# Idle products from a program constant, and three tile shapes changed, in a fused sketch-attention and ELU feed-forward kernel

## The chip, the cores and the metric

The kernel runs on one core of a Trainium2 chip. The metric is device time in microseconds of a whole execution. The kernel before took 266.83 us, the median of three runs (266.22 to 266.89).

A core has five engines that run their own instruction lists: TensorE (matrix products; PE in the profile, and PEld for its loads of the stationary operand), VectorE (DVE), ScalarE (ACT), GpSimd (POOL) and SyncE (SP), which here only issues DMAs. Semaphores order them.

## The reference

Polynomial sketch attention over 4 batches, 4 heads, 1088 positions and head size 32, then a feed-forward block of width 2048 with ELU:

```python
def phi(x):
    a = np.einsum('rd,bhsd->bhsr', S1, x)
    b = np.einsum('rd,bhsd->bhsr', S2, x)
    return np.einsum('bhsi,bhsj->bhsij', a, b).reshape(*x.shape[:-1], r * r)   # r = 8
q_p, k_p = (phi(q), phi(k))
kv = np.einsum('bhsf,bhsd->bhfd', k_p, v)
z = np.sum(k_p, axis=2)
num = np.einsum('bhsf,bhfd->bhsd', q_p, kv)
den = np.einsum('bhsf,bhf->bhs', q_p, z)[..., None] + 1e-06
attn = num / den
# x = attn with heads side by side: 4352 x 128
h = x @ w_in                                   # 4352 x 2048
g = np.where(h > 0.0, h, np.exp(np.minimum(h, 0.0)) - 1.0)
out = g @ w_out                                # 4352 x 128
```

All of it is float32 at the chip; S1, S2 and the two weight matrices arrive as 64-bit floats and are rounded to 32 bits on the chip by integer operations.

## The kernel before

**The whole.** The 4352 rows are cut into nine groups `g` of 512 rows (the last one has 256), and the hidden width into 8 pairs `cp` of 128 columns. A step `(g, cp)` computes h for one group and one pair on TensorE (`mm1`, L841), ELU on ScalarE and VectorE (`elu`), and, two steps later, the product with w_out (`mm2`, `mm2_blocks`, or `mm2_seven`, which forms a block product from seven smaller ones whose sums GpSimd makes). `steps` lists 64 such steps; the last, smaller group has a loop of its own at the end. Attention work for later groups is put between them by tables: `at(n, ...)` right behind step n's `mm1`, `mid` and `late` further behind. The order is the program's own: each engine runs its list as written, since the schedule is manual.

**Tile shapes.** TensorE's array can be used whole (128 columns of the stationary operand) or as narrower column tiles, and also cut by rows. In the profile `128*32` means 128 rows and 32 columns of the stationary operand. A float32 product appears as two matrix instructions and two loads. `quarters` (L256) issues one product as column tiles of width `width[0]`, which is 32 up to step 30 and 64 from there on; `mm2_seven` (L767) and `mm2_blocks` use the same width.

**Start.** Behind the program's opening barrier VectorE fills a tile `some` with 1.0 (L88, L89). TensorE multiplies `some` with itself into the bank `idle` in `keep_warm` (L261, L263): nothing reads the results. Three such products of 256 columns and one of 128 (L296, L297) come first. Then TensorE makes `sps` and `SXps` from the sketches Sx (L299, L285), the features of the first batch's keys `abp` (`KF`, L338), their sums `zps` (`z_tile`, L416), and the features of the first queries `abqp` (`q1_first`, L513).

**z of the first batch.** ScalarE copies the sums to `zl`. `Z` (L441) multiplies them with SXh by `quarters`, in four 32-wide tiles; VectorE masks the result into `SW` (L447). An idle product of 96 columns follows (L959), and then `zqp` (`q1z_first`, L525), which reads `SW`. From `zqp` VectorE makes the denominators and the query features (`pw`, `den`, `an`, `qp`), and goes on with rounding the first weights (`RC_2`, L193: L118, L122, L130, L138). Later batches call `Z` through `turn` (L1038).

**First feed-forward product.** TensorE transposes the query features (`qtp`), multiplies them with kv (`xps`), makes the features of the second group (`abwp`, L534), and runs an idle product of 192 columns (L974). Then `mm1_first` (L848) begins the feed-forward work with 32-wide tiles.

**Step 30.** The loop over the steps sets `width[0] = 64` ahead of step 30's `mm1` (L1103 to L1105). Behind that `mm1`, `queries(4, 6, 31)` (L699) runs products in 32*32 tiles that don't use `quarters`, and then comes `mm2_seven` of step 28.

Of the kernel before, what the change touches and what calls it, by code (L numbers as in the profile page):

```python
# [12 lines left out]
F32 = mybir.dt.float32  # L13
# [14 lines left out]
def kernel(  # L28
# [21 lines left out]
    nc = tc.nc  # L50
    B, H, S, D = q.shape
    R = S1.shape[0]
    P = 128
# [10 lines left out]
    const = ctx.enter_context(tc.tile_pool(name="const", bufs=1))  # L64
# [20 lines left out]
            src = v[b].rearrange("h (y t) d -> y h t d", t=NT)[:, :, t0:t1, :]  # L85
            eng.dma_start(vt[b][r, :VN].rearrange("p (h t d) -> p h t d", h=H, t=KT)[:, :, :t1 - t0, :], src)

    some = const.tile([P, 256], F32, name="some")  # L88
    nc.vector.memset(some[:], 1.0)  # L89
    idr = const.tile([P, 2 * R, R], F32, name="idr")  # L90
    nc.vector.memset(idr[:], 0.0)
    Sx = const.tile([P, H, D], F32, name="Sx")
# [157 lines left out]
    idle = psum.tile([P, 512], F32, name="idle", tag="o0", bufs=1)  # L250
# [2 lines left out]

    width = [32]

    def quarters(dst, lhs, rhs, **kw):  # L256
        for c in range(0, P, width[0]):
            nc.tensor.matmul(dst[c:c + width[0]], lhs[:, c:c + width[0]], rhs, skip_group_check=True,  # L258
                             tile_position=(0, c), **kw)

    def keep_warm(n, cols=256):  # L261
        for i in range(n):
            nc.tensor.matmul(idle[:, :cols], some[:, :P], some[:, :cols], skip_group_check=True)  # L263


    nc.gpsimd.tensor_copy(idr[:R], _ap(ident[:R, :R], [[0, 2 * R], [1, R]]))
# [14 lines left out]
    SXh = const.tile([P, FD], F32, name="SXh")  # L281
# [12 lines left out]
    SWq = const.tile([FD, B, 2, 4, R], F32, name="SWq")  # L294
    SWs = const.tile([FD, B - 1, 4, R], F32, name="SWs")
    keep_warm(3)  # L296
    keep_warm(1, 128)  # L297
    sps = psum.tile([P, 512], F32, name="sps", tag="aux")
    nc.tensor.matmul(sps[:, :2 * R], Sx[:].rearrange("p h d -> p (h d)"), ident[:, :2 * R])  # L299
    make_SXh()  # L300
# [102 lines left out]
    def KO_first(t0, t1):  # L403
        half, o = divmod(t0, 5)
        n = t1 - t0
        a_ = kf_ps[half][:, 64 * o:64 * (o + n)].rearrange("p (m x r) -> p m x r", x=2, r=R)[:, :, 1, :]
        b_ = feats[0][:, 0, t0:t1].rearrange("p t h r -> p (t h) r")
        nc.vector.tensor_mul(feats[0, half][:, o:o + n].rearrange("p t h i j -> p (t h) i j"),
                             _ap(a_, list(a_.ap[1:]) + [[0, R]]), _ap(b_, [[R, n * H], [0, R], [1, R]]))
# [30 lines left out]

    def Z(b, ps, zl):  # L441

        quarters(ps[:, 96:128], SXh[:], zl[:])

    def Z_out(b, ps):
        z = wzs[b] = SW[:, :, 2, :] if b == 0 else work.tile([FD, H, R], F32, name="wz", tag="wz")[:]
# [8 lines left out]
    def KV(b, ps):  # L455
        for f in range(2):
            quarters(ps[:, 128 + P * f:128 + P * f + P], kvz[b][:, f].rearrange("p c s -> p (c s)"), ident[:])
# [11 lines left out]
    def Z_first():  # L469
        ps = psum.tile([P, 512], F32, name="zps", tag="h", bufs=4)  # L470
        for i in range(KT):
            z_tile(0, ps, i)
        return ps, ZC(0, ps)
# [46 lines left out]
    def q1z_first():  # L520
        p = psum.tile([P, 512], F32, name="zqp", tag="h", bufs=4)
        for i in range(4):
            for u in range(2):
                b, t = half_tile(0, 2 * i + u)
                nc.tensor.matmul(p[64 * u:64 * u + 64, i * 32:i * 32 + 32].rearrange("p (h r) -> p h r", h=H),  # L525
                                 qT[b][:, t, :], SW[:, :, 2, :], skip_group_check=True, tile_position=(0, 64 * u))
        return p[:, :128].rearrange("p (t h r) -> p h t r", t=4, h=H)

    def q1_second():
        p = psum.tile([P, 512], F32, name="abwp", tag="h", bufs=4)  # L530
        for i in range(4):
            for u in range(2):
                b, t = half_tile(1, 2 * i + u)
                nc.tensor.matmul(p[64 * u:64 * u + 64, i * 96:i * 96 + 96], qT[b][:, t, :],  # L534
                                 SW[:].rearrange("p h x r -> p (h x r)"), skip_group_check=True,
                                 tile_position=(0, 64 * u))
        abw[1] = work.tile([P, H * 4, 3 * R], F32, name="abw1", tag="abq1", bufs=1)
        nc.scalar.copy(abw[1][:].rearrange("p (h t) y -> p h t y", h=H),
                       p[:, :384].rearrange("p (t h y) -> p h t y", t=4, h=H))
# [185 lines left out]
    def seven(g, cp):  # L725
        return 2 <= g < NQ - 1 or g == 1 and cp >= NP - 2
# [13 lines left out]
    def sums7(g, cp, c):  # L740
        if c == 0:
            ts[g, cp] = work.tile([P, 4, 2, P], F32, name="tt", tag="raw", bufs=5)
        t = ts[g, cp]
        b11, b12 = (quarter(g, cp, 0, y) for y in range(2))
        if c == 0:
            nc.gpsimd.tensor_tensor(t[:, 0], b12, b11, op=SUB)  # L746
            return
        b21, b22 = (quarter(g, cp, 1, y) for y in range(2))
        nc.gpsimd.tensor_tensor(t[:, 2], b22, b12, op=SUB)  # L749
        nc.gpsimd.tensor_tensor(t[:, 1], t[:, 2], b11, op=ADD)  # L750
        nc.gpsimd.tensor_tensor(t[:, 3], b21, t[:, 1], op=SUB)  # L751
# [40 lines left out]
    def fin_seven_copy(g):  # L792
        a = acc[g][0]
        sa = sas[g] = work.tile([P, 2, P], F32, name="sa", tag="sa", bufs=1)
        if g == 1:
            nc.scalar.copy(sa[:, 0], acc[g][1][:, :P])
            return
        nc.scalar.copy(sa[:].rearrange("p k s -> p (k s)"), a[:, P:3 * P])
# [42 lines left out]
    def mm1(g, cp, cs=(0, 1)):  # L841
        n = qn[g] * P
        if 0 in cs and (g, cp) not in hs:
            hs[g, cp] = [psum.tile([P, 512], F32, name="h", tag="h", bufs=4) for c in range(2)]
        for c in cs:
            quarters(hs[g, cp][c][:, :n], W[:, cp, c * P:c * P + P], xg[g][:, :n])

    def mm1_first():  # L848
        hs[0, 0] = [psum.tile([P, 512], F32, name="h", tag="h", bufs=4) for c in range(2)]
        for w in range(2):  # L850
            for c in range(2):
                cols = [x[:].rearrange("p (m w s) -> p w m s", w=2, s=P)[:, w] for x in (hs[0, 0][c], xg[0])]
                quarters(cols[0], W[:, 0, c * P:c * P + P], cols[1])

    def elu_a(g, cp, c, parts=(0, 1)):

        n = qn[g] * P
        if c == 0 and 0 in parts:
            es[g, cp] = work.tile([P, 2, 512], F32, name="e", tag="e", bufs=2)
        e = es[g, cp][:, c, :n]  # L860
        if 0 in parts:
            nc.scalar.activation(e, hs[g, cp][c][:, :n], RELU, scale=-1.0)  # L862
        if 1 in parts:
            nc.scalar.activation(e, e, EXP, scale=-1.0)  # L864

    def elu_d(g, cp, c):
        n = qn[g] * P
        if c == 0:
            gs[g, cp] = work.tile([P, 2, 512], F32, name="gg", tag="gg", bufs=3)
        nc.vector.scalar_tensor_tensor(gs[g, cp][:, c, :n], es[g, cp][:, c, :n], -1.0, hs[g, cp][c][:, :n],  # L870
                                       op0=ADD, op1=MAX)

    def elu(g, cp, c):
        elu_a(g, cp, c)
        elu_d(g, cp, c)

    def mm2(g, cp, first, last):
        n = qn[g] * P
        if first:
            ops[g] = psum.tile([P, 512], F32, name="o", tag=f"o{g % 2}", bufs=1)  # L880
        gg = gs.pop((g, cp))
        for c in range(2):
            quarters(ops[g][:, :n], W[:, cp, (2 + c) * P:(3 + c) * P], gg[:, c, :n],
                   start=(first and c == 0), stop=(last and c == 1))
# [66 lines left out]
    zps, zl = Z_first()  # L951
# [4 lines left out]
    Z(0, zps, zl)  # L956
    Z_out(0, zps)
    KO_first(7, KT)
    keep_warm(1, 96)  # L959
    zq = q1z_first()  # L960
    q2_den(0, zq)
    RA(0)
# [8 lines left out]
    RC_2()  # L971
    q5_early(0)
    q1_second()
    keep_warm(1, 192)  # L974
    mm1_first()
    RA(2)
    RB(2)
# [122 lines left out]
    N = len(steps)  # L1100
    for n in range(2, N):
        g, cp = steps[n]
        if n == 30:  # L1103
            width[0] = 64
        mm1(g, cp)  # L1105
        for f, *a in extra.get(n, ()):
            f(*a)
        elu(g, cp, 0)
        if seven(g, cp):
            sums7(g, cp, 0)  # L1110
        for f, *a in extra.get((n, 0), ()):
            f(*a)
        before = steps[n - 2]
        ends = n > 3 and seven(*before) and before[1] == NP - 1
        if ends:
            elu_a(g, cp, 1, (0,))
            mm2_seven(*before, False, True)
            fin_seven_copy(before[0])
            elu_a(g, cp, 1, (1,))
            fin_seven_a(before[0])  # L1120
            if before[0] == 1:
                fin_seven_b(1)
            elu_d(g, cp, 1)
        else:
            elu(g, cp, 1)
        if seven(g, cp):
            sums7(g, cp, 1)
        if ends and before[0] > 1:
            fin_seven_b(before[0])
        for f, *a in extra.get((n, 1), ()):  # L1130
            f(*a)
        g, cp = before
        if seven(g, cp):
            if cp < NP - 1:
                mm2_seven(g, cp, cp == (NP - 2 if g == 1 else 0), False)
        elif g == 1:
            mm2_blocks(cp)
        elif n > 2:
            mm2(g, cp, cp == 0, cp == NP - 1)
            if cp == NP - 1:  # L1140
                fin1(g)
# [55 lines left out]
```

## Time and profile before

| | us |
|---|---|
| median of three runs | 266.83 |
| the runs | 266.22 to 266.89 |
| profiled execution | 266.17 |
| its span, first to last instruction | 264.4 |
| TensorE busy | 258.8 (98%) |
| VectorE busy | 188.5 (71%) |
| ScalarE busy | 184.5 (70%) |
| GpSimd busy | 167.3 (63%) |
| idle products on TensorE (14 instructions) | 1.19 to about 16.3, of the span's first 16.3 |

Times in the profile count from the span's start. A line of the timeline gives start, length, engine, line of the kernel, operation, what it writes and reads, shape and count; brackets at its end tell how long the engine was idle before it and what released it. Matrix products are pipelined and their ends are modelled, so the distance between starts says more than a length. "Idle products" in this text are the ones of `keep_warm`; "idle time" is time in which an engine does nothing.

### The profile page before, as it was taken

Reading aid. Unit: us, or ns where it says so; the run is one execution under the profiler, and the core shown is the slowest. Engines: PE = TensorE matmul, PEld = TensorE weight load, DVE = VectorE, ACT = ScalarE, POOL = GpSimd, SP = SyncE. Lnnn points to the kernel's source line nnn. Section 1 sums busy time; section 2 is a strip of 40 time slices with the busy share of each in tenths; the row PEclk is TensorE's granted clock in tenths of the full one; section 3 lists DMA queues with packets and bytes.
Section 4 is the critical chain, followed back from the end, with each engine's and each line's share of the span. In section 5 each row is a group of like instructions: output and inputs, shape, how many; then the busy total and the mean of one; then the engine's idle time right before and its main releaser. Section 6 shows DMA issues by size and latency. Waiting matters only on the chain.

```text
span 264.4 us, 9711 instructions
## 1 busy us (share of the span) xinstructions
PE 258.8 (98%) x4115; PEld 160.6 (61%) x4115; DVE 188.5 (71%) x349; ACT 184.5 (70%) x356; POOL 167.3 (63%) x247
## 2 busy tenths in 40 slices
PE   8899999999999999999999999999999999999994
PEld 7652334354346666667666666665766666667994
DVE  6899999997969997996567675644446445673651
ACT  2469978677567556785587777776777777777792
POOL 4400008203279996798858799898688888998310
PEclk9999999999999999999999999999999999999999
DMA  6997089011011110001100110011001100110021
GB/s 176 333 347 212 2 252 249 6 40 49 2 22 22 29 22 2 2 4 22 26 2 0 24 22 0 2 15 29 3 2 20 24 1 2 18 17 10 2 34 28
DMA packets 26442, 13.73 MB, mean 52 GB/s; under 512 B 19328, under 2 KB 24576, under 8 KB 26400
## 3 DMA queue, kind: packets, MB, share of 16 engines
q1 hardware_dynamic: 25968, 12.76, 18.9%
q8 instruction: 32, 0.52, 0.8%
q10 hardware_dynamic: 368, 0.30, 0.3%
q14 instruction: 10, 0.08, 0.1%
q0 software_dynamic: 64, 0.07, 0.1%
HBM read 10.88 MB, written 2.23 MB: 50 GB/s over the span
## 4 chain that ended last, share of the span: by engine, by line
PE 97%; DVE 1%; ACT 0%; issue 0%; DVEq 0%
PE h L258 44%; PE pb L787 16%; PE pa L787 13%; PE o L258 5%; PE pb L763 4%; PE ol L258 3%; PE idle L263 2%; PE kv L425 1%; PE h L681 1%; PE qps L681 1%; PE kfps L357 1%; PE abp L338 1%; PE qps L573 1%; PE qtp L631 1%; PE kv L258 1%; PE xps L638 0%
## 5 line engine op out<-in xcount | busy, mean ns | idle before, releaser
L258 PE MATMUL h<-xg,W 128*32 128x512 f32 (+3 forms) x896 | 130.7, 539 | 0.0
L870 DVE SCALAR_TENSOR_TENSOR gg<-e,h 128x512 f32<-128x512 f32 x128 | 85.5, 680 | 54.3 <-ACT e L864 50.8
L862 ACT ACTIVATE e<-h 128x512 f32<-128x512 f32 x128 | 75.5, 590 | 46.4 <-PE h L258 42.7
L864 ACT ACTIVATE e<-e 128x512 f32<-128x512 f32 x128 | 80.9, 632 | 3.8
L258 PEld LDWEIGHTS h<-xg,W 128*32 128x32 f32 (+1 forms) x896 | 42.2, 122 | 43.2 <-issue 35.8
L749 POOL TENSOR_TENSOR tt<-gg 128x256 f32<-128x256 f32 x50 | 37.0, 740 | 15.4 <-DVE gg L870 15.1
L746 POOL TENSOR_TENSOR tt<-gg 128x256 f32<-128x256 f32 x50 | 36.7, 734 | 7.8 <-DVE gg L870 7.3
L750 POOL TENSOR_TENSOR tt<-tt,gg 128x256 f32<-128x256 f32 x50 | 37.5, 750 | 3.9
L751 POOL TENSOR_TENSOR tt<-gg,tt 128x256 f32<-128x256 f32 x50 | 37.1, 743 | 3.9
L787 PEld LDWEIGHTS pa<-gg,W 128*64 128x64 f32 (+1 forms) x496 | 23.8, 125 | 23.5 <-issue 22.9
L787 PE MATMUL pa<-gg,W 128*64 128x128 f32 (+1 forms) x496 | 30.5, 274 | 0.0
L787 PE MATMUL pb<-tt,SS 128*64 128x128 f32 (+1 forms) x480 | 29.5, 273 | 0.0
L787 PEld LDWEIGHTS pb<-tt,SS 128*64 128x64 f32 (+1 forms) x480 | 22.6, 126 | 0.0
L787 PE MATMUL pa<-tt,SS 128*32 128x128 f32 (+1 forms) x288 | 21.1, 273 | 0.0
L135 POOL TENSOR_TENSOR raw<-raw,tiny 128x512 f32<-128x512 f32 x1 | 1.0, 1041 | 29.9 <-DVE raw L130 29.9
L787 PE MATMUL pb<-gg,SS 128*64 128x128 f32 (+1 forms) x256 | 19.8, 273 | 0.0
L787 PE MATMUL pb<-tt,W 128*64 128x128 f32 (+1 forms) x256 | 19.8, 273 | 0.0
L258 PE MATMUL o<-gg,W 128*32 128x512 f32 x128 | 15.3, 594 | 0.0
L787 PEld LDWEIGHTS pa<-tt,SS 128*32 128x32 f32 (+1 forms) x288 | 13.5, 123 | 0.3 <-POOL tt L750 0.3
L787 PEld LDWEIGHTS pb<-gg,SS 128*64 128x64 f32 (+1 forms) x256 | 12.6, 125 | 0.0
L787 PEld LDWEIGHTS pb<-tt,W 128*64 128x64 f32 (+1 forms) x256 | 12.6, 125 | 0.0
L763 PE MATMUL pb<-gg,W 128*32 128x256 f32 x192 | 11.5, 380 | 0.0
(164 smaller groups left out, 279.6 us busy)
## 6 DMA issues: line engine op xcount, KB each, us to landing
raw<-in_moe_w_in_dram SPq DMA_DIRECT2D x8, 256.0 KB, 6.8
raw<-in_moe_w_out_dram SPq DMA_DIRECT2D x8, 256.0 KB, 6.8
hd_k<-in_k_dram SPq DMA_DIRECT2D x3, 544.0 KB, 6.8
hd_q<-in_q_dram SPq DMA_DIRECT2D x3, 544.0 KB, 8.0
out_dram<-ob SPq DMA_DIRECT2D x88, 16.0 KB, 1.5
v<-in_v_dram SPq DMA_DIRECT2D x4, 288.0 KB, 6.3
v<-in_v_dram SPq DMA_DIRECT2D x4, 256.0 KB, 8.1
hd_k<-in_k_dram SPq DMA_DIRECT2D x1, 288.0 KB, 3.4
```

What stands on the lines that cost most here:

```text
L258: nc.tensor.matmul(dst[c:c + width[0]], lhs[:, c:c + width[0]], rhs, skip_group_check=True, tile_position=(0, c), **kw)
L263: nc.tensor.matmul(idle[:, :cols], some[:, :P], some[:, :cols], skip_group_check=True)
L681: nc.tensor.matmul(ps[w][s * r:s * r + s, 64 * k:64 * (k + m)], lhs, qpT[g, i][rows, o + 2 * k:o + 2 * (k + m), f, :], start=(f == 0 and j ...
L746: nc.gpsimd.tensor_tensor(t[:, 0], b12, b11, op=SUB)
L749: nc.gpsimd.tensor_tensor(t[:, 2], b22, b12, op=SUB)
L750: nc.gpsimd.tensor_tensor(t[:, 1], t[:, 2], b11, op=ADD)
L751: nc.gpsimd.tensor_tensor(t[:, 3], b21, t[:, 1], op=SUB)
L763: nc.tensor.matmul(acc[1][0][r:r + width[0], 256 * hi:256 * hi + 256], lhs[:, w:w + width[0]], gg[:, c, 256 * u:256 * u + 256], start=(cp ...
L787: nc.tensor.matmul(bank[r:r + width[0], P * col:P * col + P], lhs[:, w:w + width[0]], rhs[:, u], start=(first and i in ((0,) if g == 1 els ...
L862: nc.scalar.activation(e, hs[g, cp][c][:, :n], RELU, scale=-1.0)
L864: nc.scalar.activation(e, e, EXP, scale=-1.0)
L870: nc.vector.scalar_tensor_tensor(gs[g, cp][:, c, :n], es[g, cp][:, c, :n], -1.0, hs[g, cp][c][:, :n], op0=ADD, op1=MAX)
```

## The change

Four edits. `some` and its memset go, and `keep_warm` reads a constant 1.0 that the program writes ahead of its opening barrier, repeated over 128 partitions and 256 columns by its access pattern. `keep_warm` gets a tile width: the 96-column product is issued in two 64-wide tiles, the 192-column product in 32-wide ones, the others as before; the last of the first four has 224 columns instead of 128. `quarters` can be given a width, and `Z` gives it 64 for the first batch. The step to `width[0] = 64` stands behind step 30's `mm1` and `queries` instead of ahead of them.

```diff
-    some = const.tile([P, 256], F32, name="some")
-    nc.vector.memset(some[:], 1.0)
...
-    def quarters(dst, lhs, rhs, **kw):
-        for c in range(0, P, width[0]):
-            nc.tensor.matmul(dst[c:c + width[0]], lhs[:, c:c + width[0]], rhs, skip_group_check=True,
+    def quarters(dst, lhs, rhs, tile=None, **kw):
+        tile = tile or width[0]
+        for c in range(0, P, tile):
+            nc.tensor.matmul(dst[c:c + tile], lhs[:, c:c + tile], rhs, skip_group_check=True,
                              tile_position=(0, c), **kw)
-    def keep_warm(n, cols=256):
+    def keep_warm(n, cols=256, tile=P):
+        ones = nc.const_aps.tensor(1.0, [P, 256], F32)
         for i in range(n):
-            nc.tensor.matmul(idle[:, :cols], some[:, :P], some[:, :cols], skip_group_check=True)
+            for c in range(0, P, tile):
+                nc.tensor.matmul(idle[c:c + tile, :cols], ones[:, :tile], ones[:, :cols], skip_group_check=True,
+                                 tile_position=(0, c))
...
     keep_warm(3)
-    keep_warm(1, 128)
+    keep_warm(1, 224)
...
-        quarters(ps[:, 96:128], SXh[:], zl[:])
+        quarters(ps[:, 96:128], SXh[:], zl[:], None if b else 64)
...
-    keep_warm(1, 96)
+    keep_warm(1, 96, 64)
...
-    keep_warm(1, 192)
+    keep_warm(1, 192, width[0])
...
-        if n == 30:
-            width[0] = 64
         mm1(g, cp)
         for f, *a in extra.get(n, ()):
             f(*a)
+        if n == 30:
+            width[0] = 64
         elu(g, cp, 0)
```

## The prediction

> **What bounds the kernel now.** I read the page's chain of waits first. By engine it is "PE 97%; DVE 1%", so TensorE sets the end. Page part 1:
>
> ```profile
> PE 258.8 (98%) x4115; PEld 160.6 (61%) x4115; DVE 188.5 (71%) x349; ACT 184.5 (70%) x356; POOL 167.3 (63%) x247
> ```
>
> Then busy time by stretches. TensorE is busy 111.59 of the 111.60 us from 16.30 to 127.90, and 4.30 of 4.30 in the next 4.30. So what arrives early at 16.3 stays early, and time taken out of TensorE's list after that is taken from the end. Before 16.3 short pieces hand over between engines, and each must be asked what released it. From the timeline of all engines, two places ahead of 16.3:
>
> ```profile
> 0.87 0.27 DVE L89 MEMSET some<- 128x256 f32 x1 [0.87 <-PEq L1182]
> 1.19 3.36 PE L263 MATMUL idle<-some 128*128 128x256 f32 x8 [1.19 <-DVE some L89]
> ...
> 4.34 0.45 PE L299 MATMUL sps<-ident,Sx 128*128 128x16 f32 x2
> ...
> 7.95 0.69 PE L513 MATMUL abqp<-Sab,qT 128*64 128x64 f32 x16
> ...
> 8.56 0.27 PE L258 MATMUL zps<-zl,SXh 128*32 128x32 f32 x8
> 8.76 0.46 PE L263 MATMUL idle<-some 128*128 128x96 f32 x2
> 8.97 0.19 DVE L447 TENSOR_TENSOR SW<-zps,bmask 128x32 f32<-128x32 f32 x1 [0.55 <-PE zps L258]
> 9.21 0.66 PE L525 MATMUL zqp<-SW,qT 128*64 128x32 f32 x16
> ```
>
> Columns: start, length, engine. Idle products wait for the memset of `some`. `sps` follows them, although its input Sx is ready at 3.71 + 0.28 = 3.99. VectorE waits 0.55 us for z, and zqp follows SW.
>
> ```profile
> 14.94 0.88 PE L534 MATMUL abwp<-SW,qT 128*64 128x96 f32 x16
> ...
> 15.39 0.69 DVE L138 SCALAR_TENSOR_TENSOR W<-raw,W 128x512 f32<-128x512 f32 x1
> ...
> 15.75 0.59 PE L263 MATMUL idle<-some 128*128 128x192 f32 x2
> ...
> 16.27 1.93 PE L258 MATMUL h<-xg,W 128*32 128x256 f32 x32
> ```
>
> The first feed-forward product (16.27) follows the idle one; its weights are rounded by 16.08. The third place is step 30, with two rows from an earlier stretch for comparison (TensorE alone):
>
> ```profile
> 35.50 1.90 PE L258 MATMUL h<-xg,W 128*32 128x512 f32 x16
> 37.33 0.71 PE L357 MATMUL kfps<-kT,Sxp 64*32 64x288 f32 x16
> ```
>
> ```profile
> 127.32 0.44 PE L787 MATMUL pa<-tt,SS 128*32 128x128 f32 x8
> 127.53 0.44 PE L787 MATMUL pb<-tt,W 128*32 128x128 f32 x8
> 127.91 1.94 PE L258 MATMUL h<-xg,W 128*64 128x512 f32 x8
> 129.77 0.41 PE L681 MATMUL h<-qpT,kvs 32*32 32x128 f32 x2
> ```
>
> Read starts, not lengths: ends overlap. Eight 128x128 products in one tile shape are 0.21 to 0.22 us start to start; the last eight before 127.91 take 0.38.
>
> **What the Trainium skill says.** "TensorEngine Tiling (Array Packing)", Key Properties: "Changing tiling mode (not just tile) drains the TensorE". It gives no price. The trace agrees and prices it: h to pb in one shape is 39.72 to 41.43 = 1.71 us, h to kfps in another shape 1.83, so 0.12. I use 0.10 where the group ahead is short, since the tiles of an h group start spread over about 0.02. "TensorE: Matmul & The Clock Gate", section What's actually happening: the clock rises after a busy window of about 3.4 us that runs free of the program. The page's clock row shows full speed from the start, so it doesn't show the rise. Durations do: loads of abp average 213 ns in 5.2 to 6.0 us and 141 ns after, and 256-column idle products last 634 ns (median, first group) against 380 at 11.6. I find no page on an operand that repeats one element.
>
> **The change part by part.**
>
> *First products.* The constant 1.0 is written at 0.28 to 0.38, before the opening barrier; other engines' first work after it starts at 0.74 to 0.87. Taking 0.78 for TensorE, the start comes 0.41 earlier. The group grows by 96 columns in each of two passes. Cold, 128 columns cost 634 - 421 = 213 ns, or 1.66 ns each; 192 cost 0.32. So `sps` moves from 4.34 to 0.78 + 3.15 + 0.32 = 4.25, by 0.09. Sab waits behind a kT transpose that starts at 4.58 on landed data, and is little earlier than 4.83, but abp (5.33) starts in the drain behind SXps and can use most of the 0.09. While the clock is still low, half of that is lost if the rise (about 6.0) stays put: 0.05. Bounds: 0 where kT's transposes (to 6.36) pace abp, 0.5 where the rise comes a window sooner. The memset off VectorE is worth nothing: the queue waits for `ident` and then for S at 2.31. If the rise came late instead, abp's pace (213 against 141 ns) would cost up to 0.9.
>
> *z in 64-wide tiles.* Neighbours abqp and zqp are 64 wide. Four shape changes (abqp, z, idle, zqp) go. The one ahead of z is on the path: 0.10. z also has four products instead of eight: about 0.02. The idle pair keeps its columns (two tiles, two passes of 96, about 0.08 each by abwp's pace of 0.81 us for eight such pairs less the drain); it would end near 8.7 and is hidden by the wait for SW, with 0.3 to spare. So SW, zqp, pw: 0.11 earlier (0.08 to 0.2). VectorE then runs unbroken from pw at 9.99 to W at 16.08, with no row released by a DMA, and carries the 0.11.
>
> *Idle 192 in 32-wide tiles.* Eight products instead of two, same columns: at h's pace (1.71 us for four rounds of 512) two rounds of 192 are 0.32, and 0.03 for the first loads. The change ahead of it remains, the one behind goes: TensorE is free at 15.75 + 0.35 = 16.10 instead of 16.27. But W ends at 16.08, and TensorE took 0.12 from VectorE's end (qp, 12.90) to its loads (13.02) at a like wait, so 16.20. Gain 0.07 (0 to 0.17) on top of the 0.11. What is late next is VectorE's rounding.
>
> *Step 30.* mm1 stays 32 wide behind 32-wide products; queries are 32*32 either way and seven-product blocks 64 wide behind them either way. Before: 127.53 to 129.77 = 2.24. After: 0.22 for the last eight, 1.83 for h with its change: 2.05. Gain 0.19 (0.09 if only one drain counts). Issue is dearer, 16 products for 8, but 1.71 to 1.72 us in both widths when no change intervenes (133.75 to 135.47 is 64 wide). The queries' data are ready: qpT at 127.15, SWs at 127.98.
>
> No part adds a wait or a DMA or passes SP's queue; one wait goes, at TensorE's first load.
>
> Sum: 0.05 + 0.11 + 0.07 + 0.19 = 0.42. The profiled execution took 266.17 (span 264.4, 1.8 around it), so 265.75 for it. It stands at the low edge of the runs, 266.22 to 266.89, which may be the clock's window falling differently. Against the median the sum gives 266.41. I take 266.25, between the two: a start 0.41 earlier also moves the whole spread of clock rises.
>
> **The rivals.**
>
> *The clock rises a window sooner (about 266.0 or less).* Speaking for it: 0.41 is 12% of a 3.4 us window, and the longer fill leaves less gap. Against: the present rise already comes 4.8 us after the start. Worth 0.4 to 0.5 more, bounded by kT's transposes: 0.9 in all, 265.3 to 266.0.
>
> *The gains don't reach the end (266.7).* W gates 16.2, ScalarE is back to back from about 20 to 30, and pb waits for its copy at 30.3. For it: that wait. Against: ScalarE's row starts behind qtp on TensorE, so it shifts too. Step 30 alone would be left, 0.1 to 0.2.
>
> *Slower: a repeated element reads slower (269.7).* `some` lies out in 256 columns, the constant is one column read with step 0. The first group is 1792 + 192 = 1984 cold columns, 3.3 us. At double price `sps` comes 3.2 us late and nothing hides it; other gains (0.37) remain, so +2.8. It decides from about 36% on: 1.2 us late, less 0.4, is 0.3% of the time. Against: 256-column products of h that read two separate pieces take 382 ns on average, contiguous idle ones 380; but no row here repeats one element.
>
> **How the numbers follow.** The measurement tells about 0.3% (0.80 us) from no change, so faster means under 266.03. Forecast 0.55, over 265.7 to 266.6, a quarter of it under 266.03; sooner clock 0.20, four fifths under; gains lost 0.17, none; slower read 0.08. Faster 0.14 + 0.16 = 0.30, slower 0.08, same 0.62. Range 265.5 to 266.9: it leaves out the slower read and the best sooner clock, about 0.12.
>
> **What would show it.** First idle load at 0.75 to 0.85, with 634 ns durations; longer ones mean the slower read. z's group at about 0.10 behind abqp's slot, no drain ahead of it; zqp 0.1 to 0.2 earlier; h behind the 192-column group at 16.0 to 16.1, released by VectorE's W; step 30's h 0.22 behind the last eight, queries 1.83 behind it. I am wrong if idle on TensorE grows after 16.3, if loads of abp turn short at another time than 6.0, or if the step-30 stretch keeps 2.24.

## The result, and the profile after

The changed kernel takes 265.87 us (median of ten runs, 265.71 to 266.23). The kernel before, run beside it, takes 266.41 us (ten runs, 266.06 to 266.89). The ratio is 0.9979, with a 95% interval of 0.9971 to 0.9988: a gain of 0.54 us, or 0.2%. The same changed kernel was run twice more among the experiments, at 0.9989 (0.9982 to 0.9997) and 0.9979 (0.9971 to 0.9988). Over all runs of both kernels, 43 after and 132 before, the medians are 265.93 and 266.32, which is 0.39 us apart. One slow run of the changed kernel, 386.65 us at a granted clock of 0.66, is not among the 43. I take 0.4 us for the size of the gain: real, and less than the 0.3% that the prediction asked for before it would speak of a change.

The profiled execution of the changed kernel took 266.23 us, the slowest of its ten, and its span is 264.4 us, exactly that of the kernel before. Read alone, the two profiles would say that nothing was gained. The lines show why they must not be read by absolute times. First the page's part 1:

```profile
PE 259.1 (98%) x4127; PEld 161.1 (61%) x4127; DVE 188.4 (71%) x348; ACT 184.3 (70%) x356; POOL 167.1 (63%) x247
```

VectorE has one instruction less (the memset) and TensorE twelve more: narrower tiles issue more products. TensorE still bounds the kernel; in the 111.63 us from its first h (16.46) to 128.09 it is busy 111.61. The timeline of all engines from 0 to 17 us (start, length, engine):

```profile
0.78 3.64 PE L265 MATMUL idle<-const-float32-1.0 128*128 128x256 f32 x8 [0.78 <-PEq L1185]
...
4.22 0.50 PE L302 MATMUL sps<-ident,Sx 128*128 128x16 f32 x2
...
8.30 0.69 PE L516 MATMUL abqp<-Sab,qT 128*64 128x64 f32 x16
...
8.81 0.26 PE L257 MATMUL zps<-zl,SXh 128*64 128x32 f32 x4
...
8.90 0.37 PE L265 MATMUL idle<-const-float32-1.0 128*64 128x96 f32 x4
...
9.19 0.19 DVE L450 TENSOR_TENSOR SW<-zps,bmask 128x32 f32<-128x32 f32 x1 [0.42 <-PE zps L257]
...
9.44 0.66 PE L528 MATMUL zqp<-SW,qT 128*64 128x32 f32 x16 [0.17 <-DVE SW L450]
...
15.17 0.88 PE L537 MATMUL abwp<-SW,qT 128*64 128x96 f32 x16
...
15.62 0.69 DVE L136 SCALAR_TENSOR_TENSOR W<-raw,W 128x512 f32<-128x512 f32 x1
...
15.98 0.54 PE L265 MATMUL idle<-const-float32-1.0 128*32 128x192 f32 x8
...
16.46 0.85 PE L257 MATMUL h<-xg,W 128*32 128x256 f32 x12
```

The first product starts at 0.78 instead of 1.19 and `sps` at 4.22 instead of 4.34. Then `abqp` starts at 8.30 instead of 7.95: 0.35 us later. Between them lie the products of `abp`, and their weight loads say what happened. Groups of weight loads by form, first of the stretch from 6.0 to 7.0 us, then from 7.0 to 7.6 (count, busy us, mean ns):

```profile
L341 PEld LDWEIGHTS abp<-Sab,kT 128*64 128x64 f32 x21 | 1.2, 203 | 0.0
...
L341 PEld LDWEIGHTS abp<-Sab,kT 128*64 128x64 f32 x13 | 0.6, 138 | 0.0
```

Before, these loads fell to 141 ns at about 6.0 us. Here they average 203 ns until 7.0 and 138 behind it. The trace keeps a record of the clock which the page's row does not resolve: it puts the rise to full speed at 5.99 us in the profile of before and at 6.91 in this one. So this execution had its clock late, and distances between neighbours have to be compared instead of times:

| stretch, start to start | before | after |
|---|---|---|
| first `abqp` to `SW` | 1.02 | 0.89 |
| first `abqp` to first h | 8.33 | 8.16 |
| last eight products to the queries, step 30 | 2.24 | 2.09 |
| first h to the queries | 113.50 | 113.35 |
| the queries to TensorE's end | 131.13 | 131.14 |

The third place is step 30, from TensorE's timeline:

```profile
127.50 0.44 PE L790 MATMUL pa<-tt,SS 128*32 128x128 f32 x8
127.72 0.44 PE L790 MATMUL pb<-tt,W 128*32 128x128 f32 x8
127.94 1.94 PE L257 MATMUL h<-xg,W 128*32 128x512 f32 x16
129.81 0.41 PE L684 MATMUL h<-qpT,kvs 32*32 32x128 f32 x2
```

The last eight products now take 127.94 - 127.72 = 0.22 us to the next group, where they took 0.38. The 0.15 gained there is the whole difference in the row from h to the queries, and the row behind it is unchanged, so in this profile nothing was given back from 16 us to the end.

### The profile page after: what moved, and what is told of

Its sections match the earlier page's. It is cut to its first block, busy times and chain, and to the rows that moved or that the text cites. A ratio compares the mean times of both kernels' runs of the same rounds, so it can differ in the third digit from the quotient of the medians.

```text
span 264.4 us, 9734 instructions
## 1 busy us (share of the span) xinstructions
PE 259.1 (98%) x4127; PEld 161.1 (61%) x4127; DVE 188.4 (71%) x348; ACT 184.3 (70%) x356; POOL 167.1 (63%) x247
## 4 chain that ended last, share of the span: by engine, by line
PE 96%; POOL 1%; DVE 1%; ACT 0%; issue 0%
PE h L257 44%; PE pb L790 16%; PE pa L790 13%; PE o L257 5%; PE pb L766 4%; PE ol L257 3%; PE idle L265 2%; PE kv L428 1%; PE h L684 1%; PE qps L684 1%; POOL kp L324 1%; PE kfps L360 1%; PE qps L576 1%; PE abp L341 1%; PE qtp L634 1%; PE kv L257 1%
```

## The experiments

**The theory.** Three small local gains (z's tiles 0.13, the first h 0.03 more, step 30 0.15) reach the end and add up; the start adds what the moment of the clock rise leaves of it. **The rivals:** the gain is the clock rising sooner and the tile shapes are worth nothing; the gains don't reach the end because VectorE's rounding or ScalarE's row holds the next thing; the idle products read differently from the constant.

### One part at a time

The start alone: the constant, and 224 columns in the last of the first four. All tile shapes stay.

```diff
-    some = const.tile([P, 256], F32, name="some")
-    nc.vector.memset(some[:], 1.0)
...
+        ones = nc.const_aps.tensor(1.0, [P, 256], F32)
-            nc.tensor.matmul(idle[:, :cols], some[:, :P], some[:, :cols], skip_group_check=True)
+            nc.tensor.matmul(idle[:, :cols], ones[:, :P], ones[:, :cols], skip_group_check=True)
...
-    keep_warm(1, 128)
+    keep_warm(1, 224)
```

> The kernel before with one part of the change: the first idle products read the program's constant, and the fourth has 224 columns. All tile shapes and step 30 as before. Theory (an early start moves the clock's rise): first idle product at 0.78, each lasting about 631 to 634 ns as with the filled tile; abp starts at 5.26 instead of 5.33; abqp to first h and step 30 (127.53 to 129.77) as before, 8.33 and 2.24 us; time 0.1 to 0.3 us less than before, with single executions spread by the moment of the rise. Rival (nothing of an early start reaches the end): within 0.05 us of before. Rival (a repeated element reads slower): idle products well over 634 ns and 0.3 us or more slower.

Measured: 266.30 us against 266.33, ratio 0.9997 (0.9988 to 1.0005). The single 256-column products last about 630 ns, as with the tile in memory (634), so the repeated element is not read slower. (Start to start says the same of the changed kernel: 1984 columns from 0.78 to 4.22 are 1.73 ns each, 1792 columns before from 1.19 to 4.34 are 1.76.) Its profile caught an early clock. Timeline of all engines, 0 to 5.3 us:

```profile
0.78 3.30 PE L262 MATMUL idle<-const-float32-1.0 128*128 128x256 f32 x8 [0.78 <-PEq L1181]
...
4.14 0.36 PE L298 MATMUL sps<-ident,Sx 128*128 128x16 f32 x2
...
4.95 0.55 PE L337 MATMUL abp<-Sab,kT 128*64 128x64 f32 x5
```

The rise is recorded at 3.59 us, and the loads of `abp` are short from the first (groups of loads, 4.9 to 8.2 us):

```profile
L337 PEld LDWEIGHTS abp<-Sab,kT 128*64 128x64 f32 x36 | 1.8, 137 | 0.4 <-DVE Sab L301 0.3
```

`abqp` starts at 7.66, which is 0.29 sooner than in the profile of before. Yet the timed runs don't show the gain of 0.1 to 0.3 that was expected: one profile with an early rise is not a faster kernel.

The tile shapes alone, with the tile `some` and its memset kept and step 30 as before. The edit is taken from the changed kernel:

```diff
+    some = const.tile([P, 256], F32, name="some")
+    nc.vector.memset(some[:], 1.0)
...
-        ones = nc.const_aps.tensor(1.0, [P, 256], F32)
+        ones = some
...
-    keep_warm(1, 224)
+    keep_warm(1, 128)
...
+        if n == 30:
+            width[0] = 64
         mm1(g, cp)
...
-        if n == 30:
-            width[0] = 64
```

> The kernel before with the tile shapes of z and of the 96- and 192-column idle products alone; the filled tile, the late start and step 30 as before. Theory (drains ahead of z and of the first h are on the path, W's rounding is the next gate): first abqp to SW 0.89 us instead of 1.02, first abqp to first h 8.16 instead of 8.33, step 30 as before 2.24; time 0.17 us less than before. Rival (gains do not reach the end, since ScalarE and a copy gate the steps around 30 us): the first h is early, but the step-30 queries are not; time as before.

Measured: 266.15 us, ratio 0.9996 (0.9989 to 1.0004). The local gain is there in full. Timeline, 7.6 to 16.6 us:

```profile
7.65 0.69 PE L518 MATMUL abqp<-Sab,qT 128*64 128x64 f32 x16
...
8.54 0.19 DVE L452 TENSOR_TENSOR SW<-zps,bmask 128x32 f32<-128x32 f32 x1 [0.34 <-PE zps L259]
...
15.34 0.53 PE L267 MATMUL idle<-some 128*32 128x192 f32 x8
...
15.81 1.07 PE L259 MATMUL h<-xg,W 128*32 128x256 f32 x16
```

`abqp` to `SW` is 0.89 and `abqp` to h is 8.16, both as in the changed kernel. But from h to the queries this execution takes 113.66 us instead of 113.50; 0.13 of the loss lies in the products of the fourth batch's kv near 118 us, with no wait that the profile names. I have no cause for it.

Step 30 alone:

```diff
-        if n == 30:
-            width[0] = 64
         mm1(g, cp)
         for f, *a in extra.get(n, ()):
             f(*a)
+        if n == 30:
+            width[0] = 64
```

> The kernel before with the width step behind step 30's queries alone. Theory (one tile change out of TensorE's list): 127.53 to 129.77 shrinks from 2.24 to 2.09, all later starts 0.15 earlier; time 0.15 us less than before. Rival (absorbed by a wait behind it): the queries start earlier, but TensorE is idle later by as much, and the time is as before.

Measured: 266.22 us, ratio 0.9997 (0.9988 to 1.0006). TensorE's timeline, 127.5 to 130.4 us:

```profile
128.04 0.44 PE L787 MATMUL pb<-tt,W 128*32 128x128 f32 x8
128.25 1.94 PE L258 MATMUL h<-xg,W 128*32 128x512 f32 x16
130.12 0.41 PE L681 MATMUL h<-qpT,kvs 32*32 32x128 f32 x2
```

130.12 - 128.04 is 2.08, against 2.24 in the kernel before: the part makes its gain alone. This execution had the latest rise of those with the first idle products, 7.07 us.

By medians the three parts give 0.03 + 0.18 + 0.11 = 0.32 us, and the whole 0.39. Each one alone is within its interval of about 0.2 us on either side, so their single times prove nothing; that the parts work is shown by the distances, and that they add up by the time of the whole.

### What a tile change costs

The changed kernel, with mm1 of steps 32 to 59 put back into 32-wide tiles among 64-wide neighbours: 55 more changes of shape, the same arithmetic.

```diff
+        if 32 <= n < 60:
+            width[0] = 32
         mm1(g, cp)
+        if 32 <= n < 60:
+            width[0] = 64
```

> The changed kernel with mm1 of steps 32 to 59 issued 32 wide and all the rest 64 wide: 27 steps get two tile changes more, one step (with queries) one more, 55 in all. Theory (each change drains TensorE and nothing covers it): at 0.095 us each, with 0.046 for the first loads of a 64-wide group as step 30 shows, 5.2 to 6.5 us slower than the changed kernel. Rival (a change costs only where TensorE has just waited, otherwise it is hidden): within 0.5 us.

Measured: 273.84 us (two runs), ratio 1.028 (1.0257 to 1.0303). That is 7.9 us more than the changed kernel, beyond the 5.2 to 6.5 that was expected: a change costs more than the price that I had put in. From the queries to TensorE's end it takes 139.05 us instead of 131.14: 7.92 us, or 0.144 us per change. One step of it in TensorE's timeline, 135 to 144 us:

```profile
136.27 0.39 PE L790 MATMUL pb<-tt,W 128*64 128x128 f32 x4
136.59 1.92 PE L257 MATMUL h<-xg,W 128*32 128x512 f32 x16
138.44 0.66 PE L790 MATMUL pa<-gg,W 128*64 128x128 f32 x8
...
140.12 1.92 PE L257 MATMUL h<-xg,W 128*32 128x512 f32 x16
```

and the same place of the changed kernel:

```profile
136.81 0.39 PE L790 MATMUL pb<-tt,W 128*64 128x128 f32 x4
137.03 1.89 PE L257 MATMUL h<-xg,W 128*64 128x512 f32 x8
138.75 0.61 PE L790 MATMUL pa<-gg,W 128*64 128x128 f32 x8
...
140.28 1.03 PE L257 MATMUL h<-xg,W 128*64 128x512 f32 x4
```

A step takes 3.53 us instead of 3.25. The change into h costs 0.32 - 0.22 = 0.10, the change out of it 1.85 - 1.72 = 0.13, and the 64-wide group behind it another 0.05 (138.44 to 138.93, the start of the group that follows `pa`, against 138.75 to 139.19). The price holds over 28 steps, and no other engine hides it.

### The start, taken away

The changed kernel without its first four idle products.

```diff
-    keep_warm(3)
-    keep_warm(1, 224)
```

> The changed kernel without its first four idle products: TensorE starts with sps at about 4.1. Theory (what counts is when TensorE gets busy): the clock rises 2.8 to 6.2 us after 4.1, so at 6.9 to 10.3, and abp runs cold: its last products are up to 1 us later; on average 3.3 us later rise times 0.43 gives 1.4 us slower than the changed kernel, 0.8 to 1.9. Rival (the start is paced by data, so cold products cost nothing): sps and all behind it 0.1 us earlier, time the same or 0.1 us less.

Measured: 267.21 us, ratio 1.0038 (1.0024 to 1.0052); against the changed kernel run beside it (265.93), 1.28 us more. TensorE's timeline, 3 to 10.6 us:

```profile
4.14 0.58 PE L300 MATMUL sps<-ident,Sx 128*128 128x16 f32 x2 [4.14 <-DVE Sx L275]
...
5.26 2.88 PE L339 MATMUL abp<-Sab,kT 128*64 128x64 f32 x36
...
8.88 1.12 PE L514 MATMUL abqp<-Sab,qT 128*64 128x64 f32 x16
```

The loads of all 36 products of `abp` are slow (groups of loads, 4.9 to 8.2 us), because the clock rises only at 10.15 us:

```profile
L339 PEld LDWEIGHTS abp<-Sab,kT 128*64 128x64 f32 x36 | 2.7, 220 | 0.2 <-DVE kT L281 0.2
```

`sps` itself starts sooner, at 4.14. First `abqp` to first h takes 8.67 us instead of 8.16, since the clock is low until 10.15; from h to the queries it is 113.34, as in the changed kernel. So the first products are worth 1.3 us, and what the trace shows of it goes through the clock.

### The moment of the rise

The changed kernel itself ran twice more beside the experiments, with no edit. The second time:

> The changed kernel once more, beside the others of this call and for one more sight of the moment at which the clock rises. Theory (the clock rises at the end of a free-running window of 3.41 us that was busy for about 0.8 of it; in the five profiles so far 2.8 to 6.1 us after the first idle product): rise between 3.6 and 7.0; first abqp at 7.65 where it comes before 5, later by 0.43 us for each us of a later rise; abqp to first h 8.16 and step 30 2.09 whatever the rise. Time 265.7 to 266.1, 0.3 to 0.6 us less than before. Rival (the two profiles of equal span are the truth, nothing was gained): time within 0.1 us of before.

and the third:

> The changed kernel again, on the same chip as the version with GpSimd. Theory: 265.7 to 266.1, the first abqp at 7.65 to 8.3 by the moment of the rise, abqp to first h 8.16, h to queries 113.36. Rival (none gained): as the kernel before.

Measured: 265.93 and 265.98 us. The distances are the same in all three profiles of the changed kernel: first `abqp` to first h 8.15 or 8.16, step 30 2.09, h to the queries 113.35, 113.36 and 113.38. Only the rise moves. Every profile, those of the experiments below too, gives one pair of rise and first `abqp`:

| kernel | first product | rise | first `abqp` |
|---|---|---|---|
| start alone | 0.78 | 3.59 | 7.66 |
| tile shapes alone | 1.19 | 4.16 | 7.65 |
| without the 192 columns | 0.78 | 4.40 | 7.72 |
| last half step on GpSimd (below) | 0.78 | 4.80 | 7.83 |
| rounding step cut (below) | 0.78 | 4.97 | 7.79 |
| 55 more shape changes | 0.78 | 5.49 | 7.73 |
| changed, second time | 0.78 | 5.71 | 7.78 |
| before | 1.19 | 5.99 | 7.95 |
| changed, third time | 0.78 | 6.56 | 8.14 |
| changed, first time | 0.78 | 6.91 | 8.30 |
| step 30 alone | 1.19 | 7.07 | 8.41 |
| without first products | none | 10.15 | 8.88 |

The same kernel rises at 5.71, 6.56 and 6.91 us. A rise up to about 5.7 gives a floor of 7.65 to 7.83; whether kT's transposes on VectorE or the loads of `abp` at full speed set it is not told apart here. From there on each us of delay costs about 0.45 us (7.78 to 8.41 for rises from 5.71 to 7.07). A start 0.41 sooner can move the spread of rises by as much. An estimate: if the rises fall evenly over 3.4 us, from 2.8 us behind the first product on, somewhat under half of them lie above the floor, and the earlier start is worth 0.41 times 0.45 for these, about 0.08 us on average. The start alone measured 0.03, which can't be told from 0.08 or from nothing.

### Is VectorE's rounding the gate?

The changed kernel without the idle product of 192 columns.

```diff
-    keep_warm(1, 192, width[0])
```

> The changed kernel without its 192-column idle products. Theory (W's rounding on VectorE gates the first h): abqp to first h stays 8.16, TensorE just waits longer there; the rest as in the changed kernel, time within 0.2 us of it. Rival (TensorE's own list gates it): first h 0.25 to 0.35 us earlier, 7.8 to 7.9 behind abqp, time 0.3 us less.

Measured: 265.87 us, ratio 0.9986 (0.9978 to 0.9994), no different from the changed kernel beside it (265.93). Timeline, 14.5 to 16.6 us:

```profile
15.03 0.69 DVE L136 SCALAR_TENSOR_TENSOR W<-raw,W 128x512 f32<-128x512 f32 x1
...
15.87 1.07 PE L257 MATMUL h<-xg,W 128*32 128x256 f32 x16 [0.40 <-DVE W L136]
```

TensorE waits 0.40 us in the place of the idle product, released by W's rounding, and `abqp` to h is 8.16 as before the edit. The gate is shown: making the idle product cheaper still would bring nothing.

### What comes behind the gate

So I opened it: the last of the four rounding steps is cut into two halves, the first of which holds the weights that the first products read. The 192 columns are left out here as well.

```diff
-            for f in (round_s, round_m, round_d, round_e):
+            for f in (round_s, round_m, round_d):
                 f(raw_2[:, :, :2 * P], W[:, :2, :2 * P])
+            for cp in range(2):
+                round_e(raw_2[:, cp, :2 * P], W[:, cp, :2 * P])
```

> The changed kernel without its 192-column idle products, and with the last rounding step of the first two weight pairs cut in two instructions, one per pair, so that the first h waits for half of it. Theory (W gates h): abqp to first h 7.85 to 7.95 instead of 8.16; if nothing behind it takes over, the step-30 queries come earlier by as much and the time is 0.2 to 0.3 us less than the changed kernel's. Rival (VectorE, longer by 0.1 us for the cut, is next: qtp or the first ELU waits): h early, but the distance from h to the queries grows by as much and the time is the changed kernel's.

Measured: 265.75 us, ratio 0.9987 (0.9977 to 0.9997). Against the changed kernel beside it this is 0.18 us less, with an interval of about 0.5 less to 0.2 more: not settled. The profile shows that h did come sooner, 14.5 to 16.6 us:

```profile
15.10 0.76 DVE L136 SCALAR_TENSOR_TENSOR W<-raw,W 128x256 f32<-128x256 f32 x2
...
15.67 1.29 PE L259 MATMUL h<-xg,W 128*32 128x256 f32 x20
```

`abqp` to h is 7.89, 0.27 less. But h to the queries is 113.69 us where the changed kernel has 113.36, so all of it is given back in this execution, at two places. The first is the next stop in line: ScalarE's copy of kv, and the products behind it (timeline, 29 to 31.5 us, with the cut):

```profile
29.41 0.35 ACT L439 COPY kvl<-kv 128x256 f32<-128x256 f32 x1
...
29.81 1.45 PEld L768 LDWEIGHTS pb<-gg,W 128*32 128x32 f32 x32 [0.90 <-ACT kvl L439]
```

and in the changed kernel:

```profile
29.56 0.35 ACT L437 COPY kvl<-kv 128x256 f32<-128x256 f32 x1
...
29.96 1.45 PEld L766 LDWEIGHTS pb<-gg,W 128*32 128x32 f32 x32 [0.81 <-ACT kvl L437]
```

These products come only 0.15 sooner, though h came 0.27 sooner. ScalarE's list waits on VectorE, which is busy without a gap from 10 to 28 us: ScalarE's part of the next weights' rounding (L106) follows an operation of VectorE and starts at 21.17 instead of 21.34, so from there on ScalarE is 0.17 ahead and no more. This place takes 0.11 us.

The second place takes more. Up to 88 us TensorE is still 0.17 ahead of the changed kernel; there its weight loads pause (timeline of the loads, 88.2 to 89 us, with the cut, then in the changed kernel):

```profile
88.59 0.26 PEld L792 LDWEIGHTS pa<-gg,W 128*32 128x32 f32 x11 [0.20 <-issue]
...
88.39 0.42 PEld L790 LDWEIGHTS pa<-gg,W 128*32 128x32 f32 x16
```

TensorE is 0.17 behind from there on, and 0.06 behind from 99 us to the queries: 0.24 us lost on balance, with no wait that the profile names. As with the 0.13 near 118 us above, I have no cause for it, and one profile can't say whether it belongs to this kernel or to this execution. So it isn't shown that a full VectorE takes back all of the gain.

Then I tried to take work from VectorE: the second half of that rounding step on GpSimd.

```diff
-            for cp in range(2):
-                round_e(raw_2[:, cp, :2 * P], W[:, cp, :2 * P])
+            round_e(raw_2[:, 1, :2 * P], W[:, 1, :2 * P], True)
+            round_e(raw_2[:, 0, :2 * P], W[:, 0, :2 * P])
```

> As the kernel with the cut rounding, but the second pair's half of the last rounding step is done by GpSimd in two operations (GpSimd has no work from 10.8 to 29 us). Theory (VectorE's full queue took the gain back): VectorE is shorter by about 0.35 us, first h again 7.85 to 7.95 behind abqp, and h to queries back near 113.36 instead of 113.69, so the queries come 0.2 to 0.3 us earlier for the same rise of the clock; time 0.2 to 0.4 us less than the changed kernel. Rival (something else that is fixed in time, a landing DMA or ScalarE's own work, is the floor): h to queries stays near 113.65 and the time is that of the changed kernel.

Measured: 266.34 us against 266.52, ratio 0.9996 (0.9987 to 1.0005); the changed kernel beside it takes 265.98. So it loses 0.36 us to the changed kernel, where 0.2 to 0.4 less was expected. First h comes 7.88 behind `abqp`, as intended, but h to the queries grows to 114.03. Timeline, 14.5 to 19.5 us:

```profile
15.19 0.85 POOL L133 TENSOR_TENSOR raw<-raw,tiny 128x256 f32<-128x256 f32 x1 [5.99 <-DVE raw L128]
...
15.48 0.71 DVE L101 TENSOR_SCALAR W<-raw 128x256 uint32<-128x256 uint32 x1
...
16.12 0.74 POOL L134 TENSOR_TENSOR W<-raw,W 128x256 f32<-128x256 f32 x1
16.13 0.87 DVE L603 TENSOR_TENSOR pw<-abw 128x128 f32<-128x128 f32 x1
...
18.90 0.63 PE L636 MATMUL qtp<-ident,qp 128*128 128x128 f32 x4 [0.40 <-DVE qp L624]
```

The same two VectorE operations in the changed kernel:

```profile
15.71 0.29 DVE L101 TENSOR_SCALAR W<-raw 128x256 uint32<-128x256 uint32 x1
...
16.08 0.29 DVE L601 TENSOR_TENSOR pw<-abw 128x128 f32<-128x128 f32 x1
```

0.29 us becomes 0.71 and 0.87 beside GpSimd: about 1.0 us is lost on VectorE where half a step of 0.4 us was to be saved, and TensorE now waits 0.40 for `qp`. The Trainium skill's "SBUF — State Buffer", section SBUF: two separate sides, says that VectorE and GpSimd share a port pair that is "an **exclusive lock**, not a bandwidth split". The trace agrees: in both pairs the GpSimd operation began first (15.19 against 15.48, 16.12 against 16.13), and the VectorE operation ends 0.14 to 0.15 us behind its end (16.19 behind 16.04, 17.00 behind 16.86).

## Why the prediction was right

The time came within 0.4 us of the forecast and inside the range. That alone says little, since the range, 265.5 to 266.9, also holds the kernel before at 266.41. What speaks for the prediction is that the distances changed at the three places and by about the sizes that it gave. Four sizes are to be mended.

- **First products.** Predicted 0.78; measured 0.78. `sps` was put at 4.25 and came at 4.22, `abp` 0.07 sooner than before. The worth of 0.05 stays open: it is below what the runs can tell, and its true form is not a fixed gain but a shift of where the rise can fall.
- **z in 64-wide tiles.** Predicted 0.11 for `abqp` to `SW`; measured 0.13. Three shape changes go (into z, out of it, and out of the idle product), not four as I counted; only the one ahead of z is on the path, so the size doesn't suffer. The idle product is hidden, as said: `zqp` waits for `SW`, not for it.
- **Idle 192.** Predicted 0.07 more, with W's rounding as the gate; measured 0.03 to 0.04 more. The gate is shown by the run without that product. From the rounding's end to h is 0.15 us (15.62 + 0.69 = 16.31 to 16.46), where I had 0.12 from another wait; that is the difference.
- **Step 30.** Predicted 0.19 as 0.22 + 1.83; measured 0.15 as 0.22 + 1.87. A shape change between h and the queries' 32*32 tiles costs 0.15 to 0.16, not the 0.12 of h and `kfps`; 55 other changes averaged 0.144.
- **The sum.** Predicted 0.42; the distances give 0.16 + 0.15 = 0.31 and whatever the start is worth, and all runs together 0.39. That 0.42 and 0.39 lie so close is partly luck: three parts were off by 0.02 to 0.04, and the 0.08 between 0.31 and 0.39 is not shown to be the start's.
- **The step that failed** is the last: "Against the median the sum gives 266.41. I take 266.25, between the two". The three runs of before held the two highest values of the ten; their median stood 0.42 above the median of the ten. The sum against 266.41 gives 265.99, and the measured time is 265.87. The sum was better than the base that I laid it on. The first reason for going below it, a base execution at the low edge, was sound; the second, that a sooner start moves the whole spread, is not shown.

The conditions for being wrong: idle time after 16.3 did not grow (111.58 us busy of 111.60 in the stretch that I had named), step 30 did not keep 2.24, but the loads of `abp` did turn short at another time than 6.0. The last was a bad sign to choose, since it differs between executions of one kernel by more than any part of the change could move it.

The rivals. *The clock a window sooner* is not how the kernel gained: the changed kernel rose at 5.71, 6.56 and 6.91, around the 5.99 of before, and the start alone measured 0.03, about 0.2 either way, where this rival asked for 0.4 to 0.5 more. *The gains don't reach the end* was wrong for this change: h to the queries fell by the 0.15 of step 30 and lost nothing. Beyond this change it becomes true in part: when h alone came 0.27 sooner, 0.11 was given back by 30 us, where ScalarE waits on VectorE. The rest of that profile's loss, near 88 us, has no cause on record. *The repeated element reads slower* is refuted, with 631 ns against 634 for a product and 1.73 against 1.76 ns for a column.

## What to carry to other kernels

Where one engine is busy without a gap, a few tenths of a us can be read off the profile by start-to-start distances at the edited place, and here they arrived at the end as long as the other full engines weren't asked to deliver sooner; each product group whose tile shape differs from both neighbours costs two changes of 0.10 to 0.16 us here, so moving a change of shape to a place that has one anyway is a gain that can be counted. When a start depends on a clock that rises at its own time, the profile of one execution is no base for absolute times. Even a distance over 100 us can be off by 0.1 to 0.2 us in one profile, as near 88 and 118 us here. Take the base time from ten runs rather than three when the effect is as small as their spread.

## What the runs showed of the hardware beyond that

The Trainium skill's "TensorE: Matmul & The Clock Gate", section What's actually happening, has the clock rise after at least one busy window of about 3.4 us, which runs free of the program. The free run is seen here: rises at 3.59 to 7.07 us in kernels that start with four idle products, and at 5.71, 6.56 and 6.91 in one and the same kernel. The length can be read too: the clock's record of full speed lasts 256.00, 259.41 or 266.24 us in the twelve profiles, which is 75, 76 and 78 times 3.413 us. A fully busy window is not needed, though. In the run with the start alone the rise came 2.81 us after the first product, which is 82% of a 3.41 us window, and with the tile shapes alone 2.97 us after it (87%). In the profile of the changed kernel a window ended 3.41 us before its rise, at 3.49 us, with 2.71 us of work in it (79%), and the clock stayed low. So, if a rise is the end of a window, the border in these traces lies between 79% and 82% of one; none of the other nine profiles speaks against it. I had taken a full window for granted and priced "a window sooner" by it; with the first products of the changed kernel, the rise came 2.8 us after the first of them in one profile and 6.1 in another.
